# A fused convolution and MLP-mixer kernel: joining additions moved in its last steps, output tiles stored as two DMAs instead of four

## The chip, the cores and the metric

The kernel runs on one core of a Trainium2 chip. The metric is the device time of one execution in microseconds (us), the median of several runs; the time before is 682.66 us (three runs, 682.52 to 683.11). The engines are named TensorE (PE in the profile; its weight loads are PEld), VectorE (DVE), ScalarE (ACT), GpSimd (POOL) and SyncE (SP). SyncE and ScalarE issue DMAs here, each in a queue of its own; the profile calls SyncE's q1 and ScalarE's q10.

## What is computed

Input and output are 2048 rows (tokens) of 512 float32 values. Cut to what matters:

```python
x  = A_u                                              # 2048 x 512
h  = x + long_convolution(layernorm(x)) + D_skip term # an S4D layer, by FFT
x1 = ln(h) + shift(gelu(ln(ln(h)) @ w1)) @ w2         # spatial-shift mixing
out = h + x1 + gelu(layernorm(x1) @ w3) @ w4          # w3: 512 x 1792, w4: 1792 x 512
```

This document is about the last line: the products with w3 (layer 3) and w4 (layer 4), the additions of their results to `h`, and the store of `h`.

## The kernel before, in words

**Where the data lies.** `h` stays in SBUF as 16 tiles: `h[:, j, :]` is tile j, 128 partitions of 512 values. Partition 32c + a of tile j holds row (4a + c) * 16 + j of the output. So the 32 partitions with one c are 32 rows of the output at a distance of 64 rows, and the next c begins 16 rows further. `ov` (line 1517) is the output seen in that way: c, a, j, d.

**Precision.** Each operand is split into a high and a low part, and each product is three matmuls (high x high, high x low, low x high). The low parts are subtractions on VectorE and GpSimd; the high parts are copies or activations on ScalarE.

**Layer 3 and 4.** The 1792 hidden columns make 14 blocks of 128. They are taken in pairs (7 pairs), and the tokens in two halves (tiles 0 to 7, tiles 8 to 15), so there are 14 steps `s` of about 20 us: steps 0 to 6 for the first half, 7 to 13 for the second. Layer 3 of a step is a 2 x 2 block product with seven multiplications instead of eight (Winograd's form of Strassen's scheme): banks `l3a`, `l3b`, `l3c`, `l3e`, `l3f`, `l3d`, `l3g`, joined on VectorE into `one`, `two`, `three`, `four`, then gelu on ScalarE. Layer 4 of a step runs one step later, while the next step's layer 3 makes new operands. In steps 0 to 6 and in the last two blocks (12 and 13) layer 4 is plain: four banks `acc0` to `acc3` (first four tiles of a half) and four banks `l_..` (the other four). In blocks 7 to 11 it too is done with seven multiplications; five of their sums are kept over the steps, in PSUM banks `res` and in SBUF tiles `held` (in the profile `xh`).

**Joining additions.** In the last step the kept sums are joined into the tiles 8 to 15 of `h`, on VectorE, two instructions for each pair of tiles: `both` (copies of two `res` banks) into columns (0, 0), `total` into `held[0]`, that into (0, 1), and so on (`adds`, line 1713; the calls in lines 1783 to 1786 and 1802). Here (q, c) means the tiles 8 + 4q to 11 + 4q and the columns 256c to 256c + 255. After them come the plain blocks' results, block 12 in `layer4b` and block 13 in the loop behind line 1814, whose addition is the last one of each tile; then the tile is stored.

**Stores.** `store(j)` (line 1576) sends tile j out in four DMAs of 32 partitions, 64 KB each. Tiles 0 to 7 go on SyncE's queue alone, in step 7 (`layer4a(6)` and `layer4b(6)`), tiles 8 to 15 on SyncE's and ScalarE's queue in turn, at the very end.

**Weights.** The split operands of w3 made in steps 0 to 6 are written to DRAM (`kept`) and read back in steps 7 to 13 (`fetch3`, line 1444) on SyncE's queue: high and low of a11 and a12 first, then the high (in step 9 `cs1w`) and low (`sn0w`) of the four sums s1 to s4, then a22. The w4 rows are read by `raw4` (line 1460), also on SyncE's queue.

**What sets the order.** Every instruction of TensorE, VectorE, ScalarE and GpSimd runs in the order in which the program text issues it (class `InOrder`; all of them have its line, L86, in the profile). SyncE's DMAs are ordered by the scheduler of the tile framework, which moves a load ahead when its buffer comes free; within the queue they start in that order.

Of the kernel before, what the change touches and what calls it, by code (L numbers as in the profile page):

```python
# [15 lines left out]
ALU = mybir.AluOpType  # L16
# [1134 lines left out]
def mixer_phase(ctx, tc, cst, h, out, finish, w3, w4):  # L1151

    nc = InOrder(tc)
# [11 lines left out]
    def slab(name):  # L1165
        return sl.tile([128, 512], F32R, tag="slab", name=name)
# [4 lines left out]
    def tmp(name):  # L1171
        return tm.tile([128, 512], F32, tag="g", name=name, bufs=5)
# [7 lines left out]
    def bank(name):  # L1180
        return ps.tile([128, 512], F32, tag="bank", name=name)
# [188 lines left out]
    half = NFT // 2  # L1370
# [73 lines left out]
    def fetch3(s):  # L1444
        one, four, last = homes3(s)
        for far, w in zip(kept[s - half], (*one, *four, last)):
            nc.sync.dma_start(w.bitcast(F32), far)
        names3(s)
# [32 lines left out]
    early, late = range(2), range(2, 4)  # L1481
# [35 lines left out]
    ov = out.rearrange("(a c j) d -> c a j d", c=4, j=16)  # L1517
    acc, H3, U, ahead = {}, {}, {}, []

    def prod(s, name, w, xk, b=None):  # L1520
        b = bank(f"l3{name}_{s}") if b is None else b
        for n, (c, wi, xi) in enumerate((c, wi, xi) for c in range(2) for wi, xi in PROD):
            nc.tensor.matmul(b, W3[s][w][wi][:, c * 128 : c * 128 + 128], XC[s // half, xk, c][xi], start=(n == 0), stop=(n == 5))
        return b

    def plus(out, b, a):
        nc.vector.tensor_tensor(out, a, b, ALU.add)
# [34 lines left out]
    def layer3b(s):  # L1562
        one, two, three, last = U.pop(s)
        low = gelu3(s, 1, 1, last)
        if s:
            plus(one, prod(s, "f", "a12", "b21"), one)
        low()
        low = gelu3(s, 0, 0, one)
        plus(three, prod(s, "d", "a22", "t4"), three)
        low()  # L1570
        low = gelu3(s, 1, 0, three)
        plus(two, prod(s, "g", "s4", "b22") if s else ahead[0], two)
        low()
        return gelu3(s, 0, 1, two)

    def store(j):
        for c in range(4):
            queue = nc.scalar if j >= 8 and c % 2 else nc.sync
            queue.dma_start(ov[c][:, j, :], h[c * 32 : c * 32 + 32, j, :])

    def layer4(s, q, i, b, first, last):
        for k in range(2):
            for n, (wi, xi) in enumerate(PROD):
                nc.tensor.matmul(b, H3[s, k, q][xi][:, i * 128 : i * 128 + 128], W4[s][k][wi],
                                 start=(first and k == 0 and n == 0), stop=(last and k == 1 and n == 2))
# [9 lines left out]
                nc.vector.scalar_tensor_tensor(h[:, j, :], h[:, j, :], off1[:, j : j + 1], acc[i], ALU.add, ALU.add)  # L1595
                store(j)

    def layer4b(s, late):
        for i in range(4):
            b = bank(f"l4_{s}_{i}")  # L1600
            layer4(s, 1, i, b, True, True)
            j = s // half * 8 + 4 + i
            if s % half == 0:
                nc.vector.scalar_tensor_tensor(h[:, j, :], h[:, j, :], off1[:, j : j + 1], b, ALU.add, ALU.add)
            else:
                nc.vector.tensor_tensor(h[:, j, :], h[:, j, :], b, ALU.add)
            if i == 0:
                late()
            if s % half == half - 1:
                store(j)  # L1610
# [6 lines left out]
    for s in range(half):  # L1617
# [27 lines left out]
        late = layer3b(s)  # L1645
# [4 lines left out]
        if s:  # L1650
            layer4b(s - 1, late)
        else:
            late()
# [13 lines left out]
    held = [[pairs(i), pairs(2 + i)] for i in range(2)]  # L1667
    OPS, B4, SRC = {}, {}, {}

    def low_of(pair, src, eng=nc.vector):  # L1670
        eng.tensor_tensor(pair[1], src, pair[0].bitcast(F32), ALU.subtract)
# [28 lines left out]
    def columns(q, c):  # L1700

        return [h[:, 8 + 4 * q + 2 * n : 10 + 4 * q + 2 * n, c * 256 : c * 256 + 256] for n in range(2)]

    two_tiles = lambda b: b.rearrange("p (t d) -> p t d", t=2)
# [8 lines left out]
    def adds(c, src):  # L1713
        for d, b in zip(columns(*c), src):
            nc.vector.tensor_tensor(d, d, b, ALU.add)
# [8 lines left out]
    def sum4(s, name, a, b, op, dst=None):  # L1724
        t = slab(f"{name}_{s}f").bitcast(F32) if dst is None else dst
        nc.vector.tensor_tensor(t, SRC[s, a], SRC[s, b], op)
        SRC[s, name], OPS[s, name] = t, SUM[name]

    cast4 = lambda s, name: nc.scalar.copy(OPS[s, name][0], SRC[s, name])
    low4 = lambda s, name, eng=nc.vector: low_of(OPS[s, name], SRC[s, name], eng)  # L1730
    fresh_banks = lambda s, name: [bank(f"l4{name}{n}_{s}") for n in range(2)]
# [3 lines left out]
    for s in range(half, 2 * half):  # L1735
        last, pre = s + 1 == 2 * half, s - 1
        summed, plain = half <= pre < end, s >= end
        if not last:
            fetch3(s + 1)
        one = slab(f"one_{s}").bitcast(F32)  # L1740
        nc.scalar.copy(one, prod(s, "a", "a11", "b11"))
        if summed:
            sum4(pre, "s1", "a21", "a22", ALU.add)
            sum4(pre, "s2", "s1", "a11", ALU.subtract)
            sum4(pre, "s3", "a11", "a21", ALU.subtract, SRC[pre, "a21"])
            for n in ("s2", "s1", "s3"):
                cast4(pre, n)
        two, three, four = (tmp(f"{n}_{s}") for n in ("two", "three", "four"))
        plus(two, prod(s, "b", "s2", "t2"), one)
        if summed:  # L1750
            sum4(pre, "s4", "a12", "s2", ALU.subtract)
            cast4(pre, "s4")
            low4(pre, "s2"), low4(pre, "s1")
        plus(three, prod(s, "c", "s3", "t3"), two)
        if summed:
            low4(pre, "s3"), low4(pre, "s4")
        b = prod(s, "e", "s1", "t1")
        plus(four, b, three)
        plus(two, b, two)
        gelus3(s, "a22", four, four)  # L1760
        low4(s, "a22", nc.gpsimd)
        plus(one, prod(s, "f", "a12", "b21"), one)
        gelus3(s, "a11", one, one)
        low4(s, "a11", nc.gpsimd)
        if summed:
            if pre == half:
                res = [wide_bank(i, f"res{i}") for i in range(4)]
            prod4(pre, "a11", "b11", res[:2], pre > half, pre + 1 == end)
            prod4(pre, "s2", "t2", res[2:], pre > half, pre + 1 == end)
            if pre + 1 == end:  # L1770
                both = [slab(f"both{i}").bitcast(F32) for i in range(2)]
                for i in range(2):
                    nc.scalar.copy(both[i], res[i])
                total = [slab(f"total{i}").bitcast(F32) for i in range(2)]
                for i in range(2):
                    nc.vector.tensor_tensor(total[i], res[2 + i], both[i], ALU.add)
        elif s == half:
            layer4a(pre)
        else:
            for i in range(4):  # L1780
                acc[i] = wide_bank(i, f"acc{pre}_{i}")
                layer4(pre, 0, i, acc[i], True, False)
            adds((0, 0), [two_tiles(b) for b in both])
            for d, b in zip(held[0], total):
                nc.vector.tensor_tensor(d, d, two_tiles(b), ALU.add)
            adds((0, 1), held[0])
        (load4 if plain else load4s)(s)
        if not last:
            raw4(s + 1)
        plus(three, prod(s, "d", "a22", "t4"), three)  # L1790
        gelus3(s, "a12", three, three)
        low4(s, "a12", nc.gpsimd)
        plus(two, prod(s, "g", "s4", "b22"), two)
        gelus3(s, "a21", two, two, plain)
        if plain:
            for k in range(2):
                for q in range(2):
                    H3[s, k, q] = OPS[s, ("a11", "a12", "a21", "a22")[2 * q + k]]
        if not summed:
            layer4b(pre, lambda: low4(s, "a21") if plain else None)  # L1800
            if s > half:
                adds((1, 1), held[0]), adds((1, 1), held[1]), adds((1, 0), held[1]), adds((1, 0), [two_tiles(b) for b in total])
            continue
        for n, x, w, c in (("v", "a12", "b21", (0, 0)), ("w", "s4", "b22", (0, 1)), ("z", "a22", "t4", (1, 0))):
            b = fresh_banks(s, n)
            prod4(pre, x, w, b)
            collect(columns(*c), b)
        for k, n, x, w in ((0, "x", "s1", "t1"), (1, "y", "s3", "t3")):
            b = fresh_banks(s, n)
            prod4(pre, x, w, b)  # L1810
            collect(held[k], b, pre == half)
        if plain:
            low4(s, "a21")
    s = 2 * half - 1
    for q in range(2):
        for i in range(4):
            b = bank(f"l4_{s}_{i}") if q else acc[i]
            layer4(s, q, i, b, q == 1, True)
            j = 8 + 4 * q + i
# [46 lines left out]
```

## Time and profile before

| | before |
|---|---|
| median of the runs | 682.66 us |
| the profiled execution: time, span | 682.68 us, 680.9 us |
| mean granted TensorE clock | 0.988 |
| busy: PE, DVE, ACT, POOL | 93%, 85%, 61%, 59% of the span |
| stores of the output | 64 DMAs of 64.0 KB: 48 on SyncE's queue, 16 on ScalarE's |

The span runs from the first instruction to the last and is 1.8 us shorter than the execution. A row of a timeline gives the start and the duration in us, the engine, the source line, the operation with what it writes and reads, how often it stands there, and in brackets the idle time before it and what ended that. A row of windows gives for a stretch each engine's busy time, the granted TensorE clock (1.00 is full speed), the mean busy share of the 16 DMA engines, and GB/s. A row of a DMA queue gives packets, MB and the share of the 16 engines' time that they took. `SPq` and `ACTq` are the DMA issues of SyncE and ScalarE.

### The profile page before, as it was taken

The page shows a single profiled execution, that of the slowest core. Times are in us where ns is not written, and L with a number is a line of the kernel's source. Part 1 is how long each engine was busy: PE and PEld are TensorE (multiplying, and loading weights), DVE is VectorE, ACT ScalarE, POOL GpSimd, SP SyncE. Part 2 cuts the span into 40 slices and gives each one's busy share as a digit, 9 for nine tenths or more (in the row PEclk, how much of TensorE's full clock was granted, in tenths as well). Part 3 has the DMA queues.
Part 4 walks back from the last instruction along what each step waited for, and adds up shares of the span by engine and source line. Part 5 has one row for each costly group of instructions (what it writes and reads, how often), then busy time and mean ns, then how long its engine had stood idle before and what let it go on. Part 6 is the DMA issues. An engine that isn't in the chain of part 4 may idle for free.

```text
span 680.9 us, 17802 instructions
## 1 busy us (share of the span) xinstructions
PE 636.5 (93%) x7224; PEld 506.8 (74%) x7224; DVE 578.5 (85%) x995; ACT 414.6 (61%) x732; POOL 400.2 (59%) x418
## 2 busy tenths in 40 slices
PE   2985999999999999999999999999999999999996
PEld 2972755673577585768888888888888889999985
DVE  6989989999998999989978799866688678898786
ACT  6998978878889886255634555544465344534430
POOL 1878489778999998402676209355511644456340
PEclk9995999999999999999999999999999999999999
DMA  8840544011301133020261524455564345333104
GB/s 212 236 176 17 158 152 132 2 49 34 65 18 34 33 95 105 9 64 1 63 200 48 169 78 148 161 182 154 191 215 139 114 152 188 120 126 123 32 0 124
DMA packets 51958, 73.58 MB, mean 108 GB/s; under 512 B 7332, under 2 KB 26788, under 8 KB 51876
## 3 DMA queue, kind: packets, MB, share of 16 engines
q1 hardware_dynamic: 50212, 69.82, 33.1%
q10 hardware_dynamic: 1152, 1.57, 0.9%
q0 software_dynamic: 512, 1.05, 0.7%
q8 instruction: 57, 0.93, 0.6%
q14 instruction: 25, 0.20, 0.1%
HBM read 44.90 MB, written 21.23 MB: 97 GB/s over the span
## 4 chain that ended last, share of the span: by engine, by line
PE 67%; ACT 12%; DVE 11%; POOL 5%; issue 4%; DMA 0%; SPq 0%; ACTq 0%; POOLq 0%; DVEq 0%
PE l L86 20%; PE bank L86 12%; PE acc L86 7%; ACT pt L86 6%; PE l3a L86 3%; PE l3d L86 3%; PE l3g L86 3%; PE l3f L86 3%; PE l3e L86 3%; PE l3c L86 3%; PE l3b L86 3%; DVE cs L86 3%; PE res L86 2%; DVE sn L86 2%; POOL pt L86 2%
## 5 line engine op out<-in xcount | busy, mean ns | idle before, releaser
L86 POOL TENSOR_TENSOR pt<-p,s 128x512 int32<-128x512 int32 x64 | 73.2, 1160 | 8.4 <-DVE sn L86 7.9
L86 ACT ACTIVATE pt<-pt 128x1056 f32<-128x1056 int32 x64 | 69.8, 1090 | 12.4 <-DVE cs L86 6.4
L86 PE MATMUL bank<-at,tbs 128*64 128x128 f32 (+1 forms) x768 | 63.1, 311 | 2.8 <-ACT u L86 0.9
L86 PEld LDWEIGHTS bank<-at,tbs 128*64 128x64 f32 x768 | 44.7, 134 | 19.0 <-ACT at L86 2.1
L86 PE MATMUL bank<-u,ms 64*128 64x128 f32 x736 | 47.5, 278 | 5.6 <-DVE u L86 1.9
L86 PEld LDWEIGHTS bank<-u,ms 64*128 64x128 f32 x736 | 43.1, 188 | 9.5 <-DVE u L86 2.6
L86 PE MATMUL bank<-cs 128*32 128x64 f32 x1024 | 33.1, 228 | 11.0 <-ACT kt L86 5.7
L86 DVE TENSOR_TENSOR cs<-pt,amx 128x512 f32<-128x512 f32 x64 | 41.1, 678 | 2.2 <-ACT amx L86 1.7
L86 PEld LDWEIGHTS bank<-cs 128*32 128x32 f32 x1024 | 24.2, 113 | 24.2 <-POOL pt L86 8.0
L86 PE MATMUL bank<-ident 128*128 128x128 f32 x292 | 39.7, 293 | 0.0
L86 ACT COPY at<-bank 128x512 f32<-128x512 f32 x44 | 27.0, 625 | 20.0 <-PE bank L86 20.0
L86 PEld LDWEIGHTS bank<-ident 128*128 128x128 f32 x292 | 36.5, 204 | 2.8 <-DVE at L86 1.1
L86 ACT ACTIVATE pt<-pt,halfpi 128x1056 f32<-128x1056 f32 x32 | 37.9, 1184 | 0.5
L86 POOL TENSOR_TENSOR cs<-pt,amp 128x512 f32<-128x512 f32 x26 | 32.0, 1230 | 5.4 <-ACT pt L86 2.9
L86 DVE STREAM_TRANSPOSE at<-bank 128x512 f32<-128x512 f32 (+1 forms) x36 | 32.8, 951 | 1.5 <-PE bank L86 1.5
L86 PE MATMUL bank<-sn 128*32 128x64 f32 x1024 | 32.5, 225 | 0.0
L86 POOL TENSOR_TENSOR sn<-pt,amp 128x512 f32<-128x512 f32 x24 | 29.6, 1235 | 4.9 <-issue 3.7
L86 DVE TENSOR_TENSOR u<-xs,bank 128x1024 f32<-128x1024 f32 x23 | 28.1, 1221 | 3.4 <-ACT xs L86 2.1
L86 DVE TENSOR_TENSOR amx<-E,amx 128x512 f32<-128x512 f32 (+1 forms) x32 | 25.3, 790 | 5.6 <-ACT amx L86 5.5
L86 POOL TENSOR_TENSOR cs0w<-raw,cs0w 128x512 fp32r<-128x512 f32 x5 | 6.5, 1303 | 36.6 <-ACT cs0w L86 36.5
L86 POOL TENSOR_TENSOR amp<-E,ec 128x512 f32<-128x512 f32 x23 | 25.3, 1106 | 4.0 <-DVE ec L86 3.5
L86 ACT ACTIVATE xq<-xq,qo,qr 128x512 f32<-128x512 f32 x15 | 11.0, 805 | 24.6 <-DVE qo L86 24.6
(1259 smaller groups left out, 2179.1 us busy)
## 6 DMA issues: line engine op xcount, KB each, us to landing
raw<-in_B_w_dram SPq DMA_DIRECT2D x28, 256.0 KB, 2.9
xq<-xq SPq DMA_DIRECT2D x72, 64.0 KB, 2.0
h<-in_A_u_dram SPq DMA_DIRECT2D x32, 128.0 KB, 4.2
h<-in_A_u_dram SPq DMA_DIRECT2D x16, 256.0 KB, 4.1
kept<-ptw SPq DMA_DIRECT2D x8, 512.0 KB, 4.3
ms<-in_mm_dram SPq DMA_DIRECT2D x4, 768.0 KB, 10.0
ptw<-kept SPq DMA_DIRECT2D x6, 512.0 KB, 5.1
out_dram<-h SPq DMA_DIRECT2D x48, 64.0 KB, 1.7
```

The source lines that it names most:

```text
L86: ins = f(*args, **kw)
```

## The change

Two things are changed. `store` sends a tile in two DMAs of 64 partitions (128 KB) instead of four of 32; on the DRAM side such a DMA walks two values of c, then 32 values of a, then a row. And the joining additions of the last step are given other places: the same fourteen instructions, in another order on VectorE.

```diff
     def store(j):
-        for c in range(4):
+        for c in range(2):
             queue = nc.scalar if j >= 8 and c % 2 else nc.sync
-            queue.dma_start(ov[c][:, j, :], h[c * 32 : c * 32 + 32, j, :])
+            queue.dma_start(ov[2 * c : 2 * c + 2, :, j, :], h[c * 64 : c * 64 + 64, j, :])
...
-    def layer4b(s, late):
+    def layer4b(s, late, between=None):
...
                 nc.vector.tensor_tensor(h[:, j, :], h[:, j, :], b, ALU.add)
+            if between:
+                between(i)
...
+    def gather(i):
+        nc.vector.tensor_tensor(held[0][i], held[0][i], two_tiles(total[i]), ALU.add)
+
+    def between(i):
+
+        nc.vector.tensor_tensor(columns(1, 0)[i % 2], columns(1, 0)[i % 2], held[1][i % 2] if i < 2 else two_tiles(total[i % 2]), ALU.add)
...
+        if last:
+            adds((0, 0), [two_tiles(b) for b in both])
         plus(two, prod(s, "b", "s2", "t2"), one)
+        if last:
+            gather(0)
...
         plus(three, prod(s, "c", "s3", "t3"), two)
+        if last:
+            gather(1)
...
-            adds((0, 0), [two_tiles(b) for b in both])
-            for d, b in zip(held[0], total):
-                nc.vector.tensor_tensor(d, d, two_tiles(b), ALU.add)
-            adds((0, 1), held[0])
+            adds((0, 1), held[0]), adds((1, 1), held[0]), adds((1, 1), held[1])
...
-            layer4b(pre, lambda: low4(s, "a21") if plain else None)
-            if s > half:
-                adds((1, 1), held[0]), adds((1, 1), held[1]), adds((1, 0), held[1]), adds((1, 0), [two_tiles(b) for b in total])
+            layer4b(pre, lambda: low4(s, "a21") if plain else None, between if last else None)
```

On SyncE's queue around the stores of tiles 0 to 7, in step 7 (`raw` are rows of w4; `cs1w` and `sn0w` are the high and low parts of the four sums for step 9, the last `sn0w` row is its a22; `ptw` and `w3s` belong to step 10), before (-) and now (+):

```order
 L1447 DMA amp0w<-kept_4108 128x512
-L1579 DMA out_dram<-h 32x512 x16
+L1579 DMA out_dram<-h 2x32x512 x8
 L1463 DMA raw_4094<-in_B_w_dram 128x512
 L1463 DMA raw_4095<-in_B_w_dram 128x512
-L1579 DMA out_dram<-h 32x512 x16
 L1447 DMA cs1w<-kept_4109 128x1024
+L1579 DMA out_dram<-h 2x32x512 x8
 L1447 DMA sn0w<-kept_4110 128x1024
 L1447 DMA sn0w<-kept_4111 128x512
```

There are half as many stores, each with an output side of 2 x 32 x 512, and `cs1w` now stands between the two groups of stores instead of behind both.

On VectorE in the last step, from the layer 3 sum `one` to the first tiles of block 13 (`xh` is `held`; `l_12_..` are block 12's results, `acc_..` block 13's), before:

```order
L86 TENSOR_TENSOR xh_6344<-xh_6344,total_7493 128x512
L86 TENSOR_TENSOR h<-h,xh_6344 128x2x256 x2
L86 TENSOR_TENSOR three_7618<-three_7618,l3d_7701 128x512
L86 TENSOR_TENSOR two_7617<-two_7617,l3g_7714 128x512
L86 TENSOR_TENSOR h<-h,l_12_0_7726 128x512
L86 TENSOR_TENSOR h_a2113l<-two_7617,h_a2113h 128x512
L86 TENSOR_TENSOR h<-h,l_12_1_7735 128x512
L86 TENSOR_TENSOR h<-h,l_12_2_7743 128x512
L86 TENSOR_TENSOR h<-h,l_12_3_7751 128x512
L86 TENSOR_TENSOR h<-h,xh_6344 128x2x256 x6
L86 TENSOR_TENSOR h<-h,total_7492 128x2x256
L86 TENSOR_TENSOR h<-h,total_7493 128x2x256
```

Eight joining additions stand behind block 12's last tile. The same place now, up to that tile and the addition behind it:

```order
L86 TENSOR_TENSOR one_7592<-one_7592,l3f_7638 128x512
L86 TENSOR_TENSOR h<-h,xh_6344 128x2x256 x6
L86 TENSOR_TENSOR three_7602<-three_7602,l3d_7689 128x512
L86 TENSOR_TENSOR two_7601<-two_7601,l3g_7702 128x512
L86 TENSOR_TENSOR h<-h,l_12_0_7714 128x512
L86 TENSOR_TENSOR h<-h,xh_6344 128x2x256
L86 TENSOR_TENSOR h_a2113l<-two_7601,h_a2113h 128x512
L86 TENSOR_TENSOR h<-h,l_12_1_7724 128x512
L86 TENSOR_TENSOR h<-h,xh_6344 128x2x256
L86 TENSOR_TENSOR h<-h,l_12_2_7733 128x512
L86 TENSOR_TENSOR h<-h,total_7476 128x2x256
L86 TENSOR_TENSOR h<-h,l_12_3_7742 128x512
```

Of the eight, four now stand in the block of six ahead of `three`, three behind block 12's first three tiles, and one (not shown) behind the fourth. The two additions of `both` and the two of `total` into `held` stand earlier, around `two` and `three`.

## The prediction

> **What bounds the kernel now.** I read the page first, then the chain that ended last, the timeline of the tail by engine, and the DMA queues. The page's busy times and two windows:
>
> ```profile
> PE 636.5 (93%) x7224; PEld 506.8 (74%) x7224; DVE 578.5 (85%) x995; ACT 414.6 (61%) x732; POOL 400.2 (59%) x418
> ...
> 600.00:620.00 20.00, 20.00 (x131) 18.32 (x131) 16.64 (x26) 9.23 (x17) 11.34 (x11) 1.00 0.38 120
> 640.00:660.00 20.00, 20.00 (x103) 17.09 (x103) 16.98 (x20) 4.61 (x8) 6.74 (x4) 1.00 0.02 8
> ```
>
> In both 20 us stretches TensorE is busy for all 20.00 at full clock; no engine makes it wait. The end of the chain, and what VectorE and the two storing queues do there (start, duration, what):
>
> ```profile
> 669.22 5.45 PE l L86 x24
> 674.68 0.02 issue
> 674.70 0.75 DVE h L86
> ...
> 664.47 3.69 DVE L86 TENSOR_TENSOR h<-h,xh 128x512 f32<-128x512 f32 x6
> 668.08 1.28 DVE L86 TENSOR_TENSOR h<-h,total 128x512 f32<-128x512 f32 x2
> 669.29 2.71 DVE L86 SCALAR_TENSOR_TENSOR h<-h,rn,acc 128x512 f32<-128x512 f32 x4
> ...
> 670.05 7.95 SPq L1579 DMA_DIRECT2D out_dram<-h  x16
> 670.05 8.11 ACTq L86 DMA_DIRECT2D out_dram<-h  x16
> ```
>
> TensorE ends at 674.68, the last addition at 675.45, the span at 680.9. VectorE starts the last eight tiles' additions at 669.29, because eight joining additions run until then; so the stores start at 670.05, need about 0.5 us per issue on each queue, and the last is issued near 678. The tail after TensorE is 680.9 - 674.7 = 6.2 us, all of it stores. The profiled execution took 682.68 us, 1.8 over its span and within 0.02 of the runs' median, 682.66. A difference under 0.2% (1.4 us) can't be told from none.
>
> **The change: the additions.** Fourteen joining additions before, fourteen after, of the same forms. Four move into gaps at 644.7 and between `two`, `three` and `four`; six stand together where six stood; four go between the last-but-one step's tile additions:
>
> ```profile
> 644.00 0.68 DVE L86 TENSOR_TENSOR h_a2112l<-two,h_a2112h 128x512 fp32r<-128x512 f32 x1
> 646.21 0.69 DVE L86 TENSOR_TENSOR two<-one,l3b 128x512 f32<-128x512 f32 x1 [1.53 <-PE l3b L86]
> ...
> 650.83 2.39 DVE L86 TENSOR_TENSOR h<-h,both 128x512 f32<-128x512 f32 x2
> 653.14 3.47 DVE L86 TENSOR_TENSOR xh<-xh,total 128x512 f32<-128x512 f32 x2
> 656.53 2.38 DVE L86 TENSOR_TENSOR h<-h,xh 128x512 f32<-128x512 f32 x2
> ...
> 662.05 0.70 DVE L86 TENSOR_TENSOR h_a2113l<-two,h_a2113h 128x512 fp32r<-128x512 f32 x1 [1.35 <-ACT two L86]
> 662.67 1.87 DVE L86 TENSOR_TENSOR h<-h,l 128x512 f32<-128x512 f32 x3
> ```
>
> Two additions of 3.69/6 = 0.62 us fit into the 1.53 us gap. The block of six takes 2.39 + 3.47 + 2.38, about 8.1 us, as now, since it is the same count at the same place; `three` after it is not later. From 662.75 on VectorE needs three tile additions (1.87) and the three joining additions left (1.8; the fourth lies in the gap ahead of 662.05, where it waits for ScalarE), and reaches the last eight tiles at 662.7 + 3.7 = 666.4 instead of 669.29. They are then gated by TensorE, and the last one still ends at 675.45. What TensorE waits for does not move, so by itself this part gives the end nothing; it starts the stores 3 us sooner, at 667.1 (one addition of 0.7 later), and would empty the queues' backlog.
>
> **The change: the stores.** Each tile goes out as two DMAs whose output side is 2 x 32 rows of 2 KB and whose SBUF side is 64 partitions. How many DMA engines take part in one? Every engine that does writes one small completion packet. Rows of the page, then of the last 17 us (packets, MB, share of 16 engines):
>
> ```profile
> DMA packets 51958, 73.58 MB, mean 108 GB/s; under 512 B 7332, under 2 KB 26788, under 8 KB 51876
> ...
> q10 hardware_dynamic: 768, 1.05, 23.9%
> q1 hardware_dynamic: 768, 1.05, 18.9%
> ...
> out_dram<-h SPq DMA_DIRECT2D x16, 64.0 KB, 1.9
> out_dram<-h ACTq DMA_DIRECT2D x16, 64.0 KB, 2.0
> ```
>
> Sixteen stores of 32 rows give 512 packets; 768 are there, so each store has 16 completions: 16 engines, two rows each. Over the whole program 7332 packets are under 512 B. Two loads go element by element (512 pieces each, of log_dt and D_skip), and the two tables fa and fi in 256 pieces of 256 B; 7332 - 1280 = 6052 are completions. The program issues 379 DMAs; with 16 each it would be 6064. Twelve are missing: one DMA ran on 4 engines. Only one in the program has an outermost count below 32, the load of D_skip, 4 x 128 single elements on both sides. Its stretch:
>
> ```profile
> 22.54 0.71 SPq L357 DMA_DIRECT2D dsk<-in_A_D_skip_dram  x1
> ...
> q1 hardware_dynamic: 519, 0.02, 27.5%
> ```
>
> Between 24.3 and 25.5 us 519 packets keep 27.5% of 16 engines busy, 4.4 engines. So a DMA is cut along its outermost count alone, though 512 pieces could have fed all. The new stores' outermost counts are 2 and 64; a cut that both sides share is 2. I take **two engines per store**, and the same two each time: no row shows which, but a cut that always begins at the same engine needs no counter.
>
> The Trainium skill says this outright ("DMA: Bandwidth & Descriptors", "Why a DMA increments its semaphore by 16 and not by 1"): the engine count is the largest number up to 16 that divides the slowest dimension of both sides, and the lowest-numbered engines are used, so all these stores would share the same two. By the same page's "Rules for kernel authors", which wants small transfers joined into large ones, the sum would be the small gain of the first rival. The trace agrees with the first as far as the D_skip load goes; no run here shows the two-sided case.
>
> **What a row costs on one engine.** Now: (18.9% + 23.9%) x 16 x 17 us over 1024 rows is 114 ns a row (SP's queue alone 100, ScalarE's 127). Below it stands the best rate of the trace:
>
> ```profile
> 36.00:38.00 2.00, 2.00 (x20) 2.00 (x19) 2.00 (x3) 1.65 (x3) 0.85 (x1) 1.00 1.06 407
> ```
>
> 407 GB/s over 16 x 1.06 is 24.0 GB/s per engine, 85 ns a row. I take 114, of the same transfers; 85 and 127 are the bounds. Eight tiles are 1024 rows, 512 per engine: **58.2 us** of work on each of two engines (43.7 to 65.0), where now 8 us suffice. It is paid twice.
>
> *The middle.* Tiles 0 to 7 are stored on SP's queue, with the weight loads of the next steps behind them:
>
> ```profile
> 533.76 8.48 SPq L1579 DMA_DIRECT2D out_dram<-h  x16
> 542.34 0.88 SPq L1463 DMA_DIRECT2D raw<-in_B_w_dram  x2
> 543.31 7.43 SPq L1579 DMA_DIRECT2D out_dram<-h  x16
> 550.85 0.38 SPq L1447 DMA_DIRECT2D cs1w<-kept  x1
> 551.32 0.87 SPq L1447 DMA_DIRECT2D sn0w<-kept  x2
> ...
> DMA to landing us min/median/max: 1.6/1.7/3.1
> ...
> 566.48 0.39 PE L86 MATMUL l3b<-t210h,sn0w 128*128 128x512 f32 x1
> ```
>
> Each load has a sixteenth of its bytes on each engine, so also on the two busy ones, behind the rows queued before it. In the new order the two `raw` loads and `cs1w` stand after eight stores and `sn0w` after all sixteen. `sn0w` is complete at 533.76 + 1.6 (a store's shortest way) + 58.2 + 4.1 (1.5 MB of loads with its own, 96 KB per engine at 24.0 GB/s) = 597.7. TensorE reads it at 566.48 and waits **31.2 us** (16.7 to 38.0). `raw` comes late as well, for ScalarE and GpSimd, but TensorE needs what they make of it only after `l3b`, so this wait covers it. The step after finds its weights there.
>
> *The clock.* After such a gap TensorE is throttled, as early in this trace:
>
> ```profile
> 50.00:54.00 4.00, 0.18 (x2) 0.00 (x0) 1.91 (x3) 3.97 (x7) 3.14 (x3) 1.00 0.00 0
> 54.00:64.00 10.00, 5.02 (x96) 2.78 (x100) 9.87 (x13) 7.58 (x19) 7.51 (x8) 0.50 0.01 2
> 64.00:68.00 4.00, 3.87 (x87) 2.05 (x86) 3.71 (x6) 3.94 (x5) 3.47 (x4) 0.54 0.22 66
> 68.00:70.00 2.00, 2.00 (x88) 1.12 (x80) 2.00 (x3) 1.97 (x5) 1.90 (x3) 1.00 0.03 8
> ```
>
> Idle from 50.2, half clock from 54, and full clock again after some 3.6 us of steady work from 64: 3.6 us at half speed lose **1.8 us** (0 to 6.8, if the whole 13.6 us stretch were worked at half).
>
> *The tail.* The first store is issued at 667.1, and the two engines are done at 667.1 + 1.6 + 58.2 = 726.9. Now the last issue ends at 678.16, so it starts near 677.7 and lands 2.0 later, and the span ends 1.2 after that; 728.1 against 680.9 is **47.2 us** (32.7 to 54.0). TensorE's last 7.6 us lie beside it and are in the sum.
>
> Sum: 31.2 + 1.8 + 47.2 = 80.2; 682.68 + 80.2 = **762.9 us**, bounds 733.9 and 776.5.
>
> **The rivals.**
> *All 16 engines (the gain).* If only the SBUF side's 64 is cut, a store is as wide as today. Then half the issues remain, the queues have no backlog, and the last pair is issued at 675.5, needs 2.0 plus 0.5 for the double size, plus 1.2: 679.2, a gain of 1.7 us, **681.0**. For it speaks that the backlog is real; against it the D_skip load, which was not spread over its inner count. It decides at once: any store with 16 completions. Chance 0.06. Were it two engines, but another pair each time, the last store's 32 rows per engine would take 3.6 us: 675.5 + 1.6 + 3.6 + 1.2 = 681.9, or 683.7 us, no measurable change; 0.03.
> *The middle is hidden.* If loads pass the stores on the two engines, only the tail is paid: 762.9 - 33.0 = **729.9** (715 at 85 ns). For: the queues show several DMAs in flight. Against: all of these sit in one queue, and the order is SP's. 0.11.
> *The two engines share one way out of SBUF.* A store of 32 partitions costs 100 to 127 ns a row where 85 is possible, so something is shared. If the two halves of a 64-partition store always collide, a row costs twice 85 and 512 take 87.4 us: the middle 60.4. In the tail SP's stores read one half of the partitions and ScalarE's the other, so there 32.7; sum 60.4 + 1.8 + 32.7 = 94.9, **777.6** (821 if the tail collides too). 0.20.
> The Trainium skill ("SBUF — State Buffer", "Door 1: The DMA port swizzle") says that partitions p and p + 32 share one port, which would make the two halves collide row by row; no row here shows it by itself.
>
> **How the numbers follow.** The forecast, two engines and both waits, has 0.60 and reaches from 734 to 776 by the price of a row. The range 728 to 800 holds it, the shared way out unless the tail collides as well, and the upper half of the hidden middle: about 0.8. Faster by over 0.2% is most of the first rival, 0.05; within 0.2% its rest and the changing pairs, 0.03; slower 0.92.
>
> **What would show it.** In the last stretch q10 has 512 + 8 x 2 = 528 packets (with 16 engines 640), DMA share about 2/16 for over 40 us, and 35 to 49 GB/s. TensorE waits in `l3b` of step 9, two steps after the one that stores tiles 0 to 7, for the DMA of `sn0w`, then runs some us at half clock. VectorE starts the last eight tiles' additions some 3 us sooner against TensorE's end. Wrong would be: a DMA share near 0.9 in the tail, no wait at `l3b`, or a time under 700.

## The result and the profile after

| | before | after |
| --- | --- | --- |
| median, us (5 runs each) | 682.66 | 734.46 |
| lowest to highest, us | 681.54 to 683.49 | 733.54 to 734.85 |
| profiled execution, us | 682.68 | 734.82 |
| its span, us | 680.9 | 733.0 |
| TensorE's last product ends, us | 674.68 | 693.72 |
| span behind it, us | 6.2 | 39.3 |

The ratio is 1.0758, 95% interval 1.0744 to 1.0771: 7.6% slower, 28.4 us less than the forecast of 762.9 and inside the range of 728 to 800. In the profiled executions the span grew by 52.1 us: 19.0 up to TensorE's end, 33.1 behind it.

The first part is one wait. The longest waits of TensorE in the changed kernel (total us, times, longest), and its products around step 9's third one:

```profile
PE l3b L86 <- DMA sn0w<-kept: 16.4, 1, 16.4
```

```profile
566.39 0.39 PE L86 MATMUL l3b<-t210h,cs1w 128*128 128x512 f32 x1
566.62 0.39 PE L86 MATMUL l3b<-t210l,cs1w 128*128 128x512 f32 x1
583.37 0.80 PE L86 MATMUL l3b<-t210h,sn0w 128*128 128x512 f32 x1 [16.37 <-DMA sn0w<-kept]
583.96 0.63 PE L86 MATMUL l3b<-t211h,cs1w 128*128 128x512 f32 x1
584.39 0.63 PE L86 MATMUL l3b<-t211l,cs1w 128*128 128x512 f32 x1
```

The wait is 16.4 us. Behind it products of this form start 0.43 us apart until 587.4, ahead of it 0.23. Of the 19.0 us, 0.4 were there before the wait (the product that waits would have come at 566.85; before the change it came at 566.48), 16.4 are the wait, and the 2.3 left are the slow products behind it.

What came ahead of `sn0w`, on SyncE's queue and in the chain that ended last:

```profile
534.12 13.36 SPq L1579 DMA_DIRECT2D out_dram<-h  x8
547.58 3.55 SPq L1463 DMA_DIRECT2D raw<-in_B_w_dram  x2
551.22 0.55 SPq L1447 DMA_DIRECT2D cs1w<-kept  x1
551.86 19.40 SPq L1579 DMA_DIRECT2D out_dram<-h  x8
571.36 3.02 SPq L1447 DMA_DIRECT2D sn0w<-kept  x2
```

```profile
571.33 0.03 issue
571.36 11.97 DMA sn0w<-kept
583.33 0.04 issue
583.37 2.08 PE l3b L86 x4
```

Sixteen stores of 64 partitions, with three loads between them, hold the queue from 534.12 to 571.26; the first `sn0w` is issued 20 us later than before (551.32) and lands 12 us after that. Most of these 12 us are the two engines again. The trace records each of a load's sixteen parts as it lands: fourteen of this `sn0w` landed from 576.2 to 577.4, the last two at 582.9 and 583.3, right behind the two parts of the last store (581.6 and 582.1). The machine meanwhile (length, busy time of TensorE, its weight loads, VectorE, ScalarE and GpSimd, granted clock, DMA share, GB/s), and in the tail:

```profile
570.00:574.00 4.00, 0.00 (x0) 0.00 (x0) 0.00 (x0) 0.59 (x2) 0.00 (x0) 0.58 0.13 51
574.00:578.00 4.00, 0.00 (x0) 0.00 (x0) 0.00 (x0) 0.00 (x0) 0.00 (x0) 0.50 0.88 296
584.00:588.00 4.00, 4.00 (x12) 3.16 (x11) 2.42 (x5) 0.62 (x1) 0.00 (x0) 0.54 0.60 183
588.00:592.00 4.00, 4.00 (x25) 3.55 (x24) 3.67 (x7) 1.46 (x3) 0.12 (x1) 1.00 0.16 36
...
700.00:710.00 10.00, 0.00 (x0) 0.00 (x0) 0.00 (x0) 0.00 (x0) 0.00 (x0) 0.50 0.13 51
```

At 570 all compute engines stand, and the DMA share is 0.13 of 16: two engines, 51 GB/s, **25.5 GB/s each**, which is 80 ns for a row of 2 KB. From 574 the loads run on the other engines as well (0.88), while the two still work off the stores until 582. From 584 to 588 the clock is 0.54 with TensorE busy throughout; from 588 it is 1.00. The tail is the same picture for 30 us: two engines, 51 GB/s, nothing else. Its two queues (packets, MB, share), and the issues:

```profile
q1 hardware_dynamic: 528, 1.05, 5.7%
q10 hardware_dynamic: 528, 1.05, 5.3%
```

```profile
686.78 24.44 SPq L1579 DMA_DIRECT2D out_dram<-h  x8
...
686.78 27.83 ACTq L86 DMA_DIRECT2D out_dram<-h  x8
```

528 = 512 rows + 8 stores x 2 completions on each queue. The tail's stores start 6.9 us ahead of TensorE's end (before: 4.6), since VectorE comes to the last eight tiles earlier against it:

```profile
669.87 8.08 DVE L86 TENSOR_TENSOR h<-h,xh 128x512 f32<-128x512 f32 x6
...
686.01 2.06 DVE L86 SCALAR_TENSOR_TENSOR h<-h,rn,acc 128x512 f32<-128x512 f32 x3
```

### The profile page after: what moved, and what is told of

The parts are those of the page before. It is cut to its first block, busy times and chain, and to the rows that moved or that the text cites. A ratio compares the mean times of both kernels' runs of the same rounds, so it can differ in the third digit from the quotient of the medians.

```text
span 733.0 us, 17770 instructions
## 1 busy us (share of the span) xinstructions
PE 640.1 (87%) x7224; PEld 508.7 (69%) x7224; DVE 582.9 (80%) x995; ACT 414.5 (57%) x732; POOL 401.3 (55%) x418
## 4 chain that ended last, share of the span: by engine, by line
PE 61%; DVE 11%; ACT 10%; POOL 5%; DMA 4%; issue 3%; SPq 1%; ACTq 0%; POOLq 0%; DVEq 0%
PE l L86 19%; PE bank L86 10%; PE acc L86 7%; ACT pt L86 6%; PE l3c L86 3%; PE l3b L86 3%; PE l3d L86 3%; PE l3e L86 3%; PE l3f L86 3%; PE l3g L86 3%; DVE cs L86 2%; PE l3a L86 2%; PE res L86 2%; DVE sn L86 2%; DMA sn0w<-kept 2%
## 5 line engine op out<-in xcount | busy, mean ns | idle before, releaser
L86 PE MATMUL bank<-cs 128*32 128x64 f32 x1024 | 33.1, 228 | 10.0 <-ACT kt L86 5.5
L86 PEld LDWEIGHTS bank<-sn 128*32 128x32 f32 x1024 | 25.3, 114 | 0.0
```

Source lines behind the costliest of these rows:

```text
L86: ins = f(*args, **kw)
```

## The experiments

In the diffs, "-" and "+" go from the changed kernel to the experiment, and "..." stands for lines left out. Ratios are to the kernel before, whose medians beside these runs were 682.60 to 682.98 us.

**1. The additions alone**, and **2. the stores alone.** Each undoes one half.

```diff
# e1_adds_only
-        for c in range(2):
+        for c in range(4):
             queue = nc.scalar if j >= 8 and c % 2 else nc.sync
-            queue.dma_start(ov[2 * c : 2 * c + 2, :, j, :], h[c * 64 : c * 64 + 64, j, :])
+            queue.dma_start(ov[c][:, j, :], h[c * 32 : c * 32 + 32, j, :])
# e2_stores_only: the kernel before, with only this loop as in the changed kernel
```

> The additions in their new places, the stores as before (four of 32 partitions). Theory (a store runs on as many DMA engines as the outermost counts of both sides share, 2 in the changed kernel, and the rows on those two engines are the whole loss): no wait at l3b of step 9, 16 completions per store, VectorE starts the last eight tiles some 3 us sooner, the queues have less backlog; 681.3 us, a gain of 1 to 2 us. Rival (the moved additions carry part of the loss, because VectorE holds TensorE up in the last step): TensorE ends later than before, over 683 us.

> The stores in two DMAs of 64 partitions, the additions where they were. Theory: both waits as in the changed kernel; the tail is the two engines' work from the first store on, and that store comes 3 us later, so 737 us. Rival (the additions carry part of the loss): below 733 us.

Measured: the additions alone 680.76 us, ratio 0.9975 (0.9966 to 0.9983); the stores alone 737.11, ratio 1.0797 (1.078 to 1.0813), with the same wait of 16.4 us in `l3b`. So the stores carry the whole loss. The additions gain 1.9 us by themselves and 2.7 under the narrow stores (737.11 - 734.46). How they do it, in the stores of the additions alone:

```profile
667.32 8.56 SPq L1579 DMA_DIRECT2D out_dram<-h  x16
```

They begin at 667.32 instead of 670.05, so the last is issued at 675.9 instead of 678.0, right behind the last addition (674.29 to 675.04): the backlog is gone.

**3. Narrow stores only in the tail**, and **4. only in the middle.** The loop of 64 partitions stays for `j >= 8`, or for `j < 8`; the other eight tiles go out as before.

```diff
+        if j >= 8:    # e4_narrow_middle: j < 8
             for c in range(2):
                 ...
+        else:
+            for c in range(4):
+                ...
```

> The changed kernel, but tiles 0 to 7 stored as before, in four DMAs of 32 partitions; only tiles 8 to 15 go on two engines. Theory (the loss has two separate places): no wait at l3b of step 9, the tail as in the changed kernel, 34.8 us longer than with the additions alone: 680.8 + 34.8 = 715.6 us. Rival (the tail is long because of what the middle left behind): under 700 us.

> The changed kernel, but tiles 8 to 15 stored as before; only tiles 0 to 7 go on two engines. Theory: the wait of 16.4 us at l3b and some 2.3 us of half clock behind it, the tail as with the additions alone: 680.8 + 18.7 = 699.5 us. Rival (the clock stays low for the rest, or later loads are late too): over 702 us.

Measured: tail alone 716.02, ratio 1.0483 (1.0466 to 1.0501), no wait in `l3b`; middle alone 700.66, ratio 1.0256 (1.024 to 1.0271). Their longest waits of TensorE, of the tail's kernel (one of an early stage, there in every kernel) and then of the middle's:

```profile
PE bank L86 <- ACT kt L86: 8.4, 5, 5.7
```

```profile
PE l3b L86 <- DMA sn0w<-kept: 16.4, 1, 16.4
```

Against the additions alone the tail costs 35.3 us (34.8 expected) and the middle 19.9 (18.7 expected; the 1.2 us more, short of the rival's 702, are not explained). The ratios add up: 0.9975 + 0.0508 + 0.0281 = 1.0764, where 1.0758 was measured for both. The two prices are separate to within the noise, and the wait belongs to the stores of tiles 0 to 7.

**5. Four engines.** One store of all 128 partitions per tile, whose output side is 4 x 32 rows.

```diff
-        for c in range(2):
-            queue = nc.scalar if j >= 8 and c % 2 else nc.sync
-            queue.dma_start(ov[2 * c : 2 * c + 2, :, j, :], h[c * 64 : c * 64 + 64, j, :])
+        queue = nc.scalar if j >= 8 and j % 2 else nc.sync
+        queue.dma_start(ov[:, :, j, :], h[:, j, :])
```

> Each tile stored in one DMA of all 128 partitions, output side 4 x 32 rows, tiles 8 to 15 on the two queues in turn. Theory: 4 engines, 4 completions per store, about 102 GB/s in the tail, 256 rows per engine and half; the scheduler puts sn0w ahead of the last four stores, so no wait in the middle; the tail is 256 x 80 ns = 20.5 us from the first store at 667.1, 9.5 us more than before: 692 us. Rival (a store costs by its size or its partitions): 256 KB are worse than 128, over 734 us. Rival (16 engines once all 128 partitions go): 681 us.

Measured: 695.61, ratio 1.0192 (1.0179 to 1.0206). Its two queues from 664 us on, and three stretches of its tail:

```profile
q1 hardware_dynamic: 528, 1.05, 11.0%
q10 hardware_dynamic: 528, 1.05, 9.0%
```

```profile
670.00:675.00 5.00, 4.83 (x22) 3.66 (x20) 2.55 (x5) 0.00 (x0) 0.00 (x0) 1.00 0.25 74
675.00:680.00 5.00, 0.00 (x0) 0.00 (x0) 0.61 (x1) 0.00 (x0) 0.00 (x0) 0.94 0.25 91
680.00:685.00 5.00, 0.00 (x0) 0.00 (x0) 0.00 (x0) 0.00 (x0) 0.00 (x0) 0.50 0.26 102
```

528 is now 512 rows + 4 stores x 4 completions. A DMA share of 0.26 is four engines, and they move 102 GB/s: 25.5 each, as with two. Twice the engines, twice the rate. TensorE has no wait for a load in step 9, but this says nothing on the engines: in this kernel the scheduler put `sn0w` (541.35) ahead of the last four stores (from 542.98). Of the 3.6 us above the expectation, about 1.9 lie from 670 to 680, where the four engines are busy and move less (74 and 91 GB/s), and 0.8 in the first store (667.88 instead of 667.1); the rest is open.

**6. The count again: 24 and 8 partitions.** If an outermost count of 64 can't use 16 engines because the other side's is 2, counts of 24 and 8 should show which number is taken. The additions are moved, tiles 0 to 7 go out in four DMAs of 32 partitions, and tiles 8 to 15 in eight DMAs each.

```diff
+            for a, n in ((0, 24), (24, 8)):
+                queue.dma_start(ov[c][a : a + n, j, :], h[c * 32 + a : c * 32 + a + n, j, :])
```

> The additions alone, but tiles 8 to 15 stored in eight DMAs each, of 24 and 8 partitions. Theory (the engine count is the largest up to 16 that divides the outermost count): 12 and 8 completions, so 80 per tile and 640 small packets in all beside 1024 rows; 32 issues per queue make the tail longer, about 686 us. Rival (a count under 16 is taken as it is, any larger one gives 16): 16 and 8 completions, 96 per tile, 768 in all.

Measured, in a single run: 685.63 us. The queues of its tail:

```profile
q10 hardware_dynamic: 832, 1.05, 20.3%
q1 hardware_dynamic: 832, 1.05, 18.3%
```

832 = 512 rows + 16 x (12 + 8) completions, and the trace's records have 12 for each store of 24 rows and 8 for each of 8. So 24 rows go to 12 engines, 8 rows to 8: the largest number up to 16 that divides the count. With 2, 4, 8, 12 and 16 engines seen, the rule of the Trainium skill that the prediction weighed ("DMA: Bandwidth & Descriptors", "Why a DMA increments its semaphore by 16 and not by 1") holds in all five cases here, the two-sided one among them.

**7. Large stores that keep 16 engines.** Two tiles go out together, 32 partitions x 4 KB, as large as the changed kernel's 128 KB and as few; the last two tiles as before.

```diff
+        elif j % 2:
+            for c in range(4):
+                queue = nc.scalar if j >= 8 and c % 2 else nc.sync
+                queue.dma_start(ov[c][:, j - 1 : j + 1, :], h[c * 32 : c * 32 + 32, j - 1 : j + 1, :])
```

> The additions in their new places; tiles 0 to 13 stored two at a time in four DMAs of 32 partitions by 4 KB (128 KB each, as large as the changed kernel's), the last two tiles as before. Theory: the outermost count is 32 on both sides, so 16 engines; no wait in the middle, no long tail; 681 us, like the additions alone. Rival (a store of 128 KB costs what it does by its size): the waits of the changed kernel stay, near 730 us.

Measured: 681.17, ratio 0.9979 (0.997 to 0.9987). Size and number of the stores cost nothing; the shape of the output side does. Nor do they gain, which fits that no backlog is left once the additions are moved. The Trainium skill ("DMA: Bandwidth & Descriptors", "Rules for kernel authors") wants many small transfers joined into a large one; here that is neutral when 16 engines are kept, 0.9979 against 0.9975.

**8. The loads of step 9 on ScalarE's queue**, and **9. on GpSimd's.** Does `sn0w` come late since it stands behind the stores in SyncE's queue, or because two engines are full whatever the queue? Three loads (`cs1w` and two of `sn0w`) are issued elsewhere.

```diff
-        for far, w in zip(kept[s - half], (*one, *four, last)):
-            nc.sync.dma_start(w.bitcast(F32), far)
+        for n, (far, w) in enumerate(zip(kept[s - half], (*one, *four, last))):
+            (nc.scalar if s == 9 and n >= 2 else nc.sync).dma_start(w.bitcast(F32), far)
# e9_loads_third_queue: nc.gpsimd instead of nc.scalar
```

> The changed kernel with three loads for step 9 (cs1w, sn0w, sn0w) issued by ScalarE instead of SyncE; same bytes, same 16 engines, the two slow ones among them. Theory (sn0w waits in SyncE's queue behind the stores, not for the two engines as such): the wait at l3b goes; step 10's loads still stand behind the stores and may cost 0 to 4 us; 734.5 - 18.7 = 715.8 us, up to 720. Rival (the two engines are taken whatever the queue): the wait stays, near 734 us.

Measured on ScalarE's queue: 729.74, ratio 1.0687 (1.0671 to 1.0703); neither expectation held. The wait in `l3b` is gone, as the theory had it, and another stands a step earlier. TensorE's longest wait, and the chain before it:

```profile
PE l3f L86 <- ACT one L86: 11.2, 1, 11.2
```

```profile
545.82 16.07 DMA out_dram<-h
561.89 0.02 issue
561.91 0.33 ACTq L86
562.24 0.04 issue
562.28 0.59 ACT one L86
562.87 0.04 issue
562.91 2.93 PE l3f L86 x6
```

ScalarE stood ahead of its second `sn0w` until a store had landed, and its own copy of `one`, next in its order, with it. In the program the DMAs of SyncE and ScalarE take eight completion signals (semaphores; the trace has their numbers) in turn, and a DMA waits until the one that had its signal last is complete; here that one was a store of the two slow engines, 16 us in flight. So the queue of a load does not free it from the stores as long as it shares their signals. The next run takes both away: the three loads issued by GpSimd have three signals of their own in its trace.

> The changed kernel, with the three loads for step 9 that TensorE needs from its third product on (cs1w and two sn0w) issued on GpSimd's queue instead of SP's: they stand neither behind the stores nor on a completion signal that a store has to give first. In the changed kernel GpSimd has no work from 544 to 554.7, so their issue fits there. Theory (the middle wait comes from the order of SP's queue and of its completion signals, and the two loaded engines still serve another queue in between): no wait of TensorE over 1 us in step 8 or 9, TensorE's end at 674.5 to 676, and the time that the narrow stores of the last eight tiles alone gave, 716.0 us (714.5 to 720; up to 4 more if GpSimd's splitting work is held behind the issue). Rival (the two engines are full of rows until about 583, whatever queue a load comes from): the wait in l3b of step 9 for sn0w stays at 10 us or more and the time at 728 to 735.

Measured: 722.77, ratio 1.0593 (1.0575 to 1.061). The loads now are issued early, on GpSimd's queue:

```profile
543.13 0.56 POOL L86 DMA_DIRECT2D cs1w<-kept  x1
543.70 1.10 POOL L86 DMA_DIRECT2D sn0w<-kept  x2
```

TensorE waits for neither, and no wait in steps 8 and 9 is over 1 us; so loads do pass the stores on the two engines, and the rival (728 to 735) falls. They are held a little all the same: the last two parts of each landed 3 to 4 us behind its other fourteen, at 549.7, 551.7 and 552.7. But the time is 6.8 us above the 716.0 of the theory and 2.8 above its 720. What is left, on SyncE's queue and in the chain:

```profile
553.48 18.48 SPq L1579 DMA_DIRECT2D out_dram<-h  x8
572.05 2.75 SPq L1447 DMA_DIRECT2D ptw<-kept  x1
...
576.83 1.64 SPq L1463 DMA_DIRECT2D raw<-in_B_w_dram  x2
```

```profile
549.88 11.65 DMA raw<-in_B_w_dram
...
561.66 2.14 POOL raws L86 x3
...
576.83 10.11 DMA raw<-in_B_w_dram
```

The next loads are late too: `raw` is issued at 576.83 (before the change at 560.51) and lands 10 us after that. TensorE has three waits in steps 9 and 10, 4.1 us together (1.0, 1.7 for `ptw`, which stood behind the stores too, and 1.4). Behind the second the granted clock was half from 589.3 to 592.7, which costs some 1.7 us more. Of the 18.4 us that the middle costs beside the narrow tail (734.46 - 716.02), 11.7 were the place of those three loads. Of the 6.8 left, 6.3 lie ahead of TensorE's end (681.94; with the narrow tail alone 675.61), and the three waits and the slow products are about 5.8 of these.

The best of all these is the additions alone, 680.76 us, 0.25% under the kernel before (interval 0.17 to 0.34%); the paired stores beside it (681.17) are no different from it.

## Why the prediction was right, and what it mis-sized

**The additions** came out as worked out: the block of six took 8.08 us (8.1), and VectorE comes to the last eight tiles 2.3 us earlier against TensorE's end, where 3 were forecast (686.01 for 693.75, before 669.29 for 674.70). That this "gives the end nothing" holds for TensorE; that the stores' backlog would go was worth 1.9 us by itself (experiment 1), which the loss covers in the whole change.

**Two engines, and the same two each time**, was right: completions of 528, a DMA share of 0.13, and 51 GB/s with many stores in flight on two queues, where changing pairs would have added up to more. Experiment 5 doubles engines and rate together. The rivals of 16 engines and of changing pairs fall with it.

**The price of a row was the step that failed in size.** The prediction took 114 ns, "of the same transfers", and kept 85 as the lower bound; 80 were measured. The 114 was the packets' busy time in the old tail, where the other engines stored too. Two microseconds of it in the kernel before:

```profile
676.00:678.00 2.00, 0.00 (x0) 0.00 (x0) 0.00 (x0) 0.00 (x0) 0.00 (x0) 1.00 0.86 264
```

That is 264 GB/s at a share of 0.86, 19 GB/s for each busy engine. Two engines alone get 25.5, four get 25.5. The price of a row on a few full engines can't be read from a stretch in which all sixteen work; the 407 GB/s row, 24.0 per engine, was the nearer one. The rest of the miss follows from this: 512 rows take 41.0 us and not 58.2. What slows a row among 16 engines (the 32 partitions they all read from, or the writing side) stays open: in experiment 6, with 12 and 8 engines on 24 and 8 partitions, it was again 114 and 127 ns (18.3% and 20.3% of 16 engines x 20 us, over 512 rows).

**The middle** was 16.4 us instead of 31.2, **the tail** 33.1 instead of 47.2, both at their lower bounds (16.7 and 32.7). That the time came out above the sum's lower bound, by 0.6 us (733.9), is luck: the bound's price of a row was too high as well, and what the two sums leave out made up for it. With 80 ns the prediction's own sum for `sn0w` is 534.1 + 1.6 + 41.0 + 4.1 = 580.8, and 583.4 was measured; the 2.6 us between are open. For the tail it is 686.8 + 1.6 + 41.0 + 1.2 = 730.6, and 733.0 was measured; most of the 2.4 us are its start:

```profile
688.00:690.00 2.00, 2.00 (x11) 1.65 (x10) 1.15 (x3) 0.00 (x0) 0.00 (x0) 1.00 0.12 16
690.00:692.00 2.00, 2.00 (x11) 1.65 (x10) 1.16 (x2) 0.00 (x0) 0.00 (x0) 1.00 0.13 42
692.00:694.00 2.00, 1.71 (x8) 1.09 (x6) 1.00 (x2) 0.00 (x0) 0.00 (x0) 1.00 0.13 45
```

The two engines are busy there, but move 16, 42 and 45 GB/s. Against 51 this loses 1.4 + 0.4 + 0.2 = 2.0 us; what holds the first rows back is not shown.

**The clock** lost 2.3 us (1.8 forecast, 0 to 6.8): it ran at half speed from 583.4 to 587.7, 4.3 us, where the early stretch showed 3.6 us of steady work.

**The hidden middle** falls by experiment 4. Its reason, "if loads pass the stores on the two engines", was half true: experiment 9 shows that they do, from another queue. Within SyncE's queue the prediction's "behind the rows queued before it" was right: the last two parts of `sn0w` landed 1.2 us behind those of the last store, and 5.9 behind its other fourteen. What it left out is that the issue stands behind the stores too (571.36), and that completion signals tie the queues together (experiment 8).

**The shared way out of SBUF** falls: two engines that read the two halves of a 64-partition store would have taken 170 ns a row if they always collided, and took 80. The rule of the Trainium skill behind it ("SBUF — State Buffer", "Door 1: The DMA port swizzle") may hold for ports; as a loss of speed it did not show at 51 GB/s, and no row shows whether the two engines read p and p + 32 at the same time.

## What to carry to other kernels

Before joining DMAs, look at the outermost count of both sides: in all stores measured here it, and not the size, said how many DMA engines worked, and packets less rows in the queue's line, divided by the number of stores, give that number. A store on few engines is paid where it is last and, through its queue and its completion signals, by the loads issued after it. Price a transfer from a stretch with as many engines at work as it will have, and keep the better rate as a bound.

## What was not expected of the hardware

The issue itself is held when few engines drain a queue. The storing issues of the changed kernel (ns: shortest, median, longest):

```profile
L1579 SPq DMA_DIRECT2D out_dram<-h x24: 511/1885/4396, 534.1 to 709.2; - x24
L86 ACTq DMA_DIRECT2D out_dram<-h x8: 575/1372/4574, 686.8 to 713.4; - x8
```

Before, the median on SyncE was 420 ns. A store gives each of its two engines 32 rows, 2.6 us at 80 ns, and in the middle the second eight took 19.40 / 8 = 2.4 us each to issue: the queue takes new work at the speed at which old work leaves. The completion signals are not the reason: those of the first eight stores were free from 535.0 on, and the last three of the eight still took 2.4 to 2.9 us each. In the tail both queues feed the same two engines, and an issue takes up to 4.6 us. An engine with other work, as ScalarE has a step earlier, would presumably stand as long; no run here shows it.
